# The first unit's row maxima moved from GpSimd to VectorE, sent in two transfers instead of four, and four max products moved behind the start of the attention loop

## The chip, the cores and the metric

The kernel runs on one NeuronCore of a Trainium2 chip. Its engines are TensorE (PE; PEld is its weight load), VectorE (DVE), ScalarE (ACT), GpSimd (POOL) and SyncE (SP), which here only issues DMA transfers. The metric is the device time of one execution in microseconds: the median of the timed runs.

## The reference

A transformer block whose two normalizations are modulated by a condition vector. 2048 rows of 512 numbers, 32 heads of 16 numbers, one key and one value head shared by all of them, and an MLP of width 1376:

```python
mod = silu(c) @ w_mod                       # sa, ca, ga, sb, cb, gb
h = layernorm(x) * (1 + ca) + sa
q, k, v = h @ wq, h @ wk, h @ wv            # k and v have one head
p = softmax(einsum("bhqd,bkd->bhqk", q, k) * Dh ** -0.5)
x = x + ga * (einsum("bhqk,bkd->bhqd", p, v) @ wo)
h = layernorm(x) * (1 + cb) + sb
x = x + gb * (gelu(h @ w1 + b1) @ w2 + b2)
```

## The kernel before, in words

**Units.** The 2048 query rows are cut into 8 blocks of 256, the 32 heads into 8 groups of 4. A block and a group are a *unit*; there are 64, and a block's 8 units come one after the other (`units`, line 469). The queries of unit u lie in one of four buffers `qst` (`load_q`, line 473, brings them with eight transfers; six for the first four units). The partitions 0 to 63 of the buffer hold two heads (s = 0), the partitions 64 to 127 the other two (s = 1), so that two products run beside each other on the two halves of the array.

**Max products.** The softmax subtracts each row's maximum within the score product itself: two partitions of each half of `qst` (48, 49 and 112, 113) hold the negated share of the maxima, high and low part, against keys' rows that hold -1. So the maxima have to be known before a unit's score products. For them the scores are computed a first time: `Max.step` (line 505) issues one product of 128 queries with 512 keys into a bank of PSUM `m` (three banks in turn) and VectorE reduces it to one maximum per row (line 517). A unit has 32 such products; the two halves s have lists of their own. When the last one of a unit is reduced, `put_max` (line 536) lets VectorE reduce over the four key blocks and transpose (lines 565 and 566), GpSimd arrange the turned numbers in rows (four small operations, line 560) and split them into a high and a low part (lines 133 and 140), and sends the four rows into `qst` (line 555).

**Prologue.** Normalization, keys, values and the first queries are computed for all rows. Max products of units 0 and 1 are put between the other products by the table `SLOTS`: each entry gives a number of products and the names of jobs behind them (`rows`: modulation rows on TensorE; `wq n`: a quarter of the query weights split by ScalarE and GpSimd, `prep_wq`, line 336; `load`: `load_q(2)`). `FIRST_MAX` is the order of the first products; unit 0's 48th in that order is its last. While the prologue runs, whatever is put off with `later` is done at once. Then `while mp.done < lead[0]` adds products until `lead[0]` = 32 + 4 * `LEAD_0` are done, and `keep_warm(WARM[3])` adds idle products, which nobody reads.

**Loop.** Each unit has eight steps K, taken in pairs: an iteration has a step X = K and a step Y = K + 1. In the first half the score products of X are mixed with max products of later units and, if there is one, with a batch of another job (late query projections, and later the output projection and the MLP); the second half does the same for Y. `sexp` (line 597) computes a score product into one of three banks `e` and ScalarE takes its exponential; `pv` (line 629) multiplies by the values into the bank `v`. Where there is a batch, the first half takes max products of s = 1, the second those of s = 0. A counter `clock` goes up by four in an iteration, so by 16 in a unit: two counts after each half step. Jobs put off with `later(n, fn)` are issued when it has moved on by n: the maxima's reduction at the next count that is 1 mod 4, the gather one count later, the transfers four counts after the reduction (`MAX_WAIT`). Preparation of weights (`prep_w1` and others: load, split on GpSimd, store through SyncE) takes a step at each iteration's end.

**How many max products.** `lead[u]` is how many are to be done when unit u begins: 32 * (u + 1) + 24 from unit 8 on, and in a straight line from `lead[0]` to `lead[8]` before. Each iteration issues the even number that comes nearest to the line: 8 in all iterations before the change. `load_q(u + 1)` is issued as soon as half of unit u's products are reduced.

**Order.** Every engine, SyncE too, executes its instructions in the order in which the program issues them. An instruction that waits holds all behind it on that engine.

Of the kernel before, what the change touches and what calls it, by code (L numbers as in the profile page):

```python
# [14 lines left out]
P = 128  # L15
# [4 lines left out]
GELU_R = 0.044715 ** 0.5  # L20

LEAD = 6
LEAD_0 = 6
FIRST_MAX = ((0, 0), (1, 0), (0, 1), (1, 1), (0, 2), (0, 3), (1, 2), (1, 3))
SLOTS = ((2, "keys 1", "keys 1"), (2, "keys 1", "keys 1"), (2, "low 1", "heads 2"), (2, "heads 2", "k 1"), (1, "warm"), (1, "heads 2"), (2, "heads 2", "v 0"),
# [4 lines left out]
MAX_WAIT = (1, 4)  # L30
QBUFS = 4
PREP = 4
# [9 lines left out]
SOON = 6  # L42
GROUP = 4
NORM_WAIT = 6
WARM = (4, 16, 2, 5)
MOD_WAIT = 3
AHEAD = 4.5

# [1 line left out]
def raw(ap):  # L50
    return ap.bitcast(F32)
# [3 lines left out]
def adaln_mqa_mlp(  # L55
# [15 lines left out]
    nc = tc.nc  # L71
# [25 lines left out]
    def pad(pool, nbytes, name):  # L97

        nc.gpsimd.memset(pool.tile([P, nbytes // 4], F32, name=name), 0.0)
# [27 lines left out]
    def ebank():  # L127
        turns[0] += 1
        return dict(tag=f"e{turns[0] % 3}", bufs=1)

    def split(dst_h, dst_l, src, eng_h, eng_l, between=None):
        if eng_h is nc.gpsimd:
            eng_h.tensor_scalar(out=dst_h, in0=src, scalar1=1.0, scalar2=0.0, op0=ALU.mult, op1=ALU.add)
        elif eng_h is nc.scalar:
            eng_h.copy(dst_h, src)
        else:
            eng_h.tensor_copy(out=dst_h, in_=src)
        if between:
            between()
        eng_l.tensor_tensor(out=dst_l, in0=src, in1=raw(dst_h), op=ALU.subtract)  # L140
# [7 lines left out]
    def later(n, fn):  # L148
        if draining[0]:
            fn()  # L150
        else:
            pending.append((clock[0] + n, fn))
# [130 lines left out]

    idles = []

    def keep_warm(n, **place):

        for k in range(n):
            if k == 0 or not place:
                ps = psum.tile([P, BQ], F32, name=f"idle{len(idles)}", **(place or dict(tag="m", bufs=3)))  # L290
                idles.append(ps)
            nc.tensor.matmul(ps, wkH[:, 0, :], wkH.rearrange("p k n -> p (k n)"), start=True, stop=True)

    def mod_rows(ps, k, wm):

# [19 lines left out]
    wkH = pro.tile([P, KD, P], F32R, name="wkH")  # L315
# [32 lines left out]
    bigH = att.tile([P, NB - 1, KD, BQ], F32R, name="bigH", tag="bigH")  # L348
# [8 lines left out]
    def stats1(b, between=None):  # L357
        mv, rs = ln_stats(xts[b], pro, QT, between)
        nm = pro.tile([P, QT], F32, name=f"nm{b}", tag="nm", bufs=2)
        if b:  # L360
            nc.gpsimd.tensor_tensor(out=nm, in0=mv[:, :, 0], in1=rs, op=ALU.mult)
            nc.gpsimd.tensor_scalar(out=nm, in0=nm, scalar1=-1.0, scalar2=0.0, op0=ALU.mult, op1=ALU.add)
        hts_stats[b] = mv, rs, nm

    def xhat1(b, eng):

        mv, rs, nm = hts_stats[b]
        xt = xts[b]
        for t in range(QT):
            if eng is nc.scalar:  # L370
                nc.scalar.activation(xt[:, t, :], xt[:, t, :], AF.Identity, scale=rs[:, t:t + 1], bias=nm[:, t:t + 1])
            else:
                eng.tensor_scalar(out=xt[:, t, :], in0=xt[:, t, :], scalar1=mv[:, t, 0:1], scalar2=rs[:, t:t + 1],
                                  op0=ALU.subtract, op1=ALU.mult)
            yield

    def turn1(b, d):
        ps = psum.tile([P, BQ], F32, name=f"tp{b}_{d}", **ebank())
        for t in range(QT):
            nc.tensor.transpose(ps[:, t * P:(t + 1) * P], xts[b][:, t, d * P:(d + 1) * P], ident)  # L380
        tps[b, d] = ps

    def mod1(b, d, eng_h, eng_l, between=None):
        hH, hL = hts[b]
        h32 = pro.tile([P, BQ], F32, name=f"h32_{b}_{d}", tag="h32", bufs=4)
        nc.scalar.activation(h32, tps.pop((b, d)), AF.Identity, scale=ca1[:, d:d + 1], bias=sa[:, d:d + 1])
        split(hH[:, d, :], hL[:, d, :], h32, eng_h, eng_l, between)
# [142 lines left out]
    placed = set()  # L530
# [5 lines left out]
    def put_max(u, mx):  # L536

        T = blocks[units[u][0]][1] // P  # L540
        qst = qsts[u]
        mm = mms[u % 2]
        turned = att.tile([P, 32], F32, name=f"turned{u}", tag="turned", bufs=2)
        if u == 0:
            pad(att, 256, "pad7")
        mt = att.tile([4 * T, P], F32, name=f"mt{u}", tag="mt", bufs=2)
        mh = att.tile([4 * T, P], F32R, name=f"mh{u}", tag="mh", bufs=2)
        ml = att.tile([4 * T, P], F32R, name=f"ml{u}", tag="ml", bufs=2)

        def send():  # L550
            for s in range(2):
                for r, src in ((48, mh), (49, ml)):
                    dst = qst[64 * s + r:64 * s + r + 1].rearrange("p j (t n) -> p (j t) n", n=P)
                    ring = nc.scalar if u == 0 and s else nc.sync
                    ring.dma_start(out=raw(dst), in_=raw(src[2 * T * s:2 * T * (s + 1), :].unsqueeze(1)))
            placed.add(u)

        def gather():
            for g in range(0, P, 32):
                nc.gpsimd.tensor_scalar(out=mt[:, g:g + 32], in0=turned[g:g + 4 * T, :], scalar1=1.0, scalar2=0.0,  # L560
                                        op0=ALU.mult, op1=ALU.add)
            split(mh, ml, mt, nc.gpsimd, nc.gpsimd)

        def reduce():
            nc.vector.tensor_reduce(out=mm[:, :4 * T], in_=mx, axis=AX.X, op=ALU.max)
            nc.vector.transpose(out=turned, in_=mm)  # L566
            later(MAX_WAIT[0], gather)
            later(MAX_WAIT[1], send)


        if NQ <= u < NQ + 2:
            reduce()
        else:
            later((0 - clock[0]) % 4 + 1, reduce)
# [661 lines left out]
    first = [sum(size[:u]) for u in range(NU + 1)]  # L1236
    mp = Max()

    def chunk(n):
        for _ in range(n):  # L1240
            mp.step(mp.done % 2)

    act, dve, pool = nc.scalar, nc.vector, nc.gpsimd

# [16 lines left out]
    def run(job, n=99):  # L1261
        for _ in range(n):
            if next(job, True):
                return

    def heads(b):

        for d in range(KD):
            turn1(b, d)
            mod1(b, d, pool if d == 1 else act, dve if b == 1 and d > 1 else pool)  # L1270
            if (b, d) == (2, KD - 1):
                load_mods(3)
            yield

    def keys(b):
        for i, _ in enumerate(kv_products(b)):
            if i == KD - 1:
                kv_out(b)
            yield
# [8 lines left out]
    def q_group():  # L1288
        for i in range(KD):
            next(projections[0])  # L1290
            if i == KD - 1:
                next(projections.pop(0))
            yield

    def warm():
        keep_warm(WARM[2], tag="x")
        yield

    def one(fn, *args):
        fn(*args)  # L1300
        yield
# [13 lines left out]
    turn1(0, 3)  # L1315
    keep_warm(WARM[0])
    mod1(0, 1, pool, dve, lambda: stats1(1))
# [3 lines left out]
    rows = xhat1(1, act)  # L1321
# [17 lines left out]
    def last_h(t):  # L1339
        if t == QT - 1:  # L1340
# [5 lines left out]
    run(xhat1(2, act))  # L1346
    run(xhat1(3, pool))
    keep_warm(WARM[1])
    work = {"keys 1": keys(1), "heads 2": heads(2), "heads 3": heads(3), "q 1": q_group(), "keys 2": keys(2), "keys 3": keys(3),
            "v 0": one(v_out, 0), "v 1": one(v_out, 1), "v 2": one(v_out, 2), "v 3": one(v_out, 3), "rows": late_rows(),  # L1350
            "low 1": one(low_k, 1), "low 2": one(low_k, 2), "low 3": one(low_k, 3), "k 1": one(repeat_k, 1), "k 2": one(repeat_k, 2), "k 3": one(repeat_k, 3), "load": one(load_q, 2), "warm": warm(),
            "wq 1": one(prep_wq, 1), "wq 2": one(prep_wq, 2), "wq 3": one(prep_wq, 3)}
    for n, *names in SLOTS:
        chunk(n)
        for name in names:
            next(work[name])
    assert 0 in placed and len(mods_late) == KD
    draining[0] = False
    nc.gpsimd.tensor_scalar(out=b1r, in0=b1c, scalar1=GELU_R, scalar2=0.0, op0=ALU.mult, op1=ALU.add)
# [9 lines left out]
    for u in range(NQ):  # L1369
        lead[u] = min(first[1] + 4 * LEAD_0 + (lead[NQ] - first[1] - 4 * LEAD_0) * u / NQ, first[u + QBUFS - 1] - 2)  # L1370

# [35 lines left out]
            if units[u][1] == NQ - 1:  # L1407
                put_off(rest(units[u][0], units[u][0] == len(blocks) - 1))

    keep_warm(WARM[3], tag="e2", bufs=1)  # L1410
    behind = None
    bare = [False]
    for u in range(NU):
        for K in range(0, steps[u], 2):
            goal = lead[u] + (lead[u + 1] - lead[u]) * (K + 2) / steps[u]
            goal = min(goal, first[u + QBUFS] if u + QBUFS < NU else first[NU])
            n = max(0, 2 * round((goal - mp.done) / 2))
# [165 lines left out]
```

## Time and profile before

| | |
|---|---|
| timed runs, us | 1556.4, 1556.62, 1558.17 (median 1556.62) |
| profiled execution, us | 1555.99 |
| its span, us | 1554.1 |
| granted TensorE clock | 1.0 |
| TensorE busy | 1537.9 us, 99% |
| VectorE busy | 1398.3 us, 90% |
| ScalarE busy | 1230.4 us, 79% |
| GpSimd busy | 683.7 us, 44% |
| first score product of the loop | at 75.14 us |

The span goes from the first to the last instruction of the profiled execution; the execution's time is a little longer. A row of the timeline gives start and length in us, engine, line, operation, output and inputs with sizes and the number of instructions merged; in brackets stands how long the engine was idle before and what ended that. SPq and ACTq are transfers issued by SyncE and ScalarE. Rows of the table by stretches give the busy time of PE, PEld, DVE, ACT and POOL (with the number of instructions), then the granted clock, the share of time in which the DMA engines were busy, and GB/s.

### The profile page before, as it was taken

Reading aid. Unit: us, or ns where it says so; the run is one execution under the profiler, and the core shown is the slowest. Engines: PE = TensorE matmul, PEld = TensorE weight load, DVE = VectorE, ACT = ScalarE, POOL = GpSimd, SP = SyncE. Lnnn points to the kernel's source line nnn. Section 1 sums busy time; section 2 is a strip of 40 time slices with the busy share of each in tenths; the row PEclk is TensorE's granted clock in tenths of the full one; section 3 lists DMA queues with packets and bytes.
Section 4 is the critical chain, followed back from the end, with each engine's and each line's share of the span. In section 5 each row is a group of like instructions: output and inputs, shape, how many; then the busy total and the mean of one; then the engine's idle time right before and its main releaser. Section 6 shows DMA issues by size and latency. Waiting matters only on the chain.

```text
span 1554.1 us, 41556 instructions
## 1 busy us (share of the span) xinstructions
PE 1537.9 (99%) x16405; PEld 954.4 (61%) x16405; DVE 1398.3 (90%) x2488; ACT 1230.4 (79%) x2401; POOL 683.7 (44%) x1206
## 2 busy tenths in 40 slices
PE   7999999999999999999999999999999999999999
PEld 4455555567655665557655676556655676566658
DVE  7999999999999999999999999999999999999814
ACT  5577778788877887788877888788877888778874
POOL 5535432867422571246521563235711574046511
PEclk9999999999999999999999999999999999999999
DMA  7226412413030220303112120302212230203141
GB/s 240 102 89 199 151 57 81 130 51 97 18 105 26 72 68 28 103 19 109 33 51 79 56 87 16 111 26 88 68 30 73 60 101 25 87 28 99 48 150 48
DMA packets 84215, 120.85 MB, mean 78 GB/s; under 512 B 21342, under 2 KB 57438, under 8 KB 83764
## 3 DMA queue, kind: packets, MB, share of 16 engines
q1 hardware_dynamic: 84004, 118.18, 23.7%
q8 instruction: 130, 2.13, 0.6%
q14 instruction: 65, 0.53, 0.1%
q10 hardware_dynamic: 16, 0.00, 0.0%
HBM read 90.87 MB, written 26.74 MB: 76 GB/s over the span
## 4 chain that ended last, share of the span: by engine, by line
PE 86%; DVE 8%; issue 3%; POOL 2%; DMA 1%; ACT 0%; SPq 0%; POOLq 0%; DVEq 0%
PE acc L638 29%; PE m L512 23%; PE e L617 16%; PE w1ps L198 8%; DVE mx L517 6%; PE w2ps L198 2%; PE w2ps L188 2%; DMA xt<-in_A_x_dram 1%; PE w1ps L188 1%; PE wops L198 1%; PE tp L198 1%; PE qps L198 1%; PE kps L165 1%; DVE st L823 0%; DVE x L816 0%
## 5 line engine op out<-in xcount | busy, mean ns | idle before, releaser
L517 DVE TENSOR_REDUCE mx<-m 128x1 f32<-128x512 f32 x2048 | 1270.6, 682 | 86.6 <-PE m L512 65.1
L621 ACT ACTIVATE p<-e 128x512 f32<-128x512 f32 x2048 | 1098.8, 598 | 255.1 <-PE e L617 112.0
L512 PE MATMUL m<-ks,qst 64*128 64x512 f32 x2048 | 836.7, 429 | 2.0 <-DVE mx L517 0.6
L617 PE MATMUL e<-qst,ks 64*128 64x512 f32 x2048 | 740.2, 412 | 0.0
L638 PE MATMUL acc<-p,va 128*32 128x256 f32 x8192 | 548.0, 385 | 0.0
L512 PEld LDWEIGHTS m<-ks,qst 64*128 64x128 f32 x2048 | 368.2, 184 | 205.1 <-DVE mx L517 173.5
L617 PEld LDWEIGHTS e<-qst,ks 64*128 64x128 f32 x2048 | 359.6, 184 | 89.3 <-ACT p L621 62.5
L638 PEld LDWEIGHTS acc<-p,va 128*32 128x32 f32 x8192 | 214.0, 109 | 213.9 <-issue 110.9
L198 PE MATMUL w1ps<-h2H,w1t 64*128 64x256 f32 x1232 | 235.5, 287 | 0.0
L560 POOL TENSOR_SCALAR mt<-turned 8x32 f32<-8x32 f32 x256 | 53.1, 208 | 399.9 <-DVE turned L566 387.9
L198 PEld LDWEIGHTS w1ps<-h2H,w1t 64*128 64x128 f32 x1232 | 186.0, 185 | 28.9 <-DVE mx L517 14.8
L198 PE MATMUL w1ps<-h2L,w1t 64*128 64x256 f32 x616 | 169.3, 275 | 0.0
L198 PE MATMUL w2ps<-w2H,gH 64*128 64x512 f32 x274 | 120.3, 439 | 0.0
L198 PEld LDWEIGHTS w1ps<-h2L,w1t 64*128 64x128 f32 x616 | 114.1, 185 | 0.0
L198 PE MATMUL w2ps<-w2L,gH 64*128 64x512 f32 x274 | 107.5, 392 | 0.0
L198 PE MATMUL w2ps<-w2H,gL 64*128 64x512 f32 x274 | 106.9, 390 | 0.0
L975 POOL TENSOR_SCALAR tt<-tt 128x256 f32<-128x256 f32 x77 | 31.0, 402 | 131.5 <-ACT tt L974 96.5
L140 POOL TENSOR_TENSOR gL<-z,gH 128x256 fp32r<-128x256 f32 x77 | 57.0, 741 | 6.4
L976 POOL TENSOR_TENSOR tt<-tt,z 128x256 f32<-128x256 f32 x77 | 56.7, 736 | 6.4
L986 POOL TENSOR_TENSOR z<-tt,z 128x256 f32<-128x256 f32 x77 | 56.4, 732 | 6.0
L985 POOL TENSOR_TENSOR tt<-tt,z 128x256 f32<-128x256 f32 x77 | 56.5, 733 | 0.0
L198 PEld LDWEIGHTS w2ps<-w2H,gH 64*128 64x128 f32 x274 | 50.4, 184 | 6.7 <-DVE ot L1038 2.5
(193 smaller groups left out, 1503.5 us busy)
## 6 DMA issues: line engine op xcount, KB each, us to landing
w1t<-dw SPq DMA_DIRECT2D x82, 512.0 KB
qst<-dq SPq DMA_DIRECT2D x384, 32.0 KB
do<-oc SPq DMA_DIRECT2D x62, 128.0 KB
dw<-w1s SPq DMA_DIRECT2D x11, 512.0 KB
xt<-in_A_x_dram SPq DMA_DIRECT2D x4, 1024.0 KB
dq<-qH SPq DMA_DIRECT2D x16, 256.0 KB
dq<-qL SPq DMA_DIRECT2D x16, 256.0 KB
x<-in_A_x_dram SPq DMA_DIRECT2D x8, 512.0 KB
```

Of the source, the lines that this page charges most:

```text
L140: eng_l.tensor_tensor(out=dst_l, in0=src, in1=raw(dst_h), op=ALU.subtract)
L188: nc.tensor.matmul(ps, a, b_, start=first_, stop=last_)
L198: ins = nc.tensor.matmul(ps, a[rows], b_[rows], start=first_ and s == 0, stop=last_ and s == 1)
L512: nc.tensor.matmul(m, qsts[u][rows, j, t * P:(t + 1) * P], ks[rows, kc * 512:(kc + 1) * 512], start=True, stop=True)
L517: nc.vector.tensor_reduce(out=self.mx[u][:, i, kc:kc + 1], in_=m, axis=AX.X, op=ALU.max)
L560: nc.gpsimd.tensor_scalar(out=mt[:, g:g + 32], in0=turned[g:g + 4 * T, :], scalar1=1.0, scalar2=0.0, op0=ALU.mult, op1=ALU.add)
L617: nc.tensor.matmul(e, ks[rows, kt * P:(kt + 1) * P], rhs, start=True, stop=True)
L621: ins = nc.scalar.activation(dst, e, AF.Exp, scale=0.25)
L638: ins = nc.tensor.matmul(accs[u][32 * cidx:32 * cidx + 32, :], va[:, kt, :], rhs, start=kt == 0, stop=kt == NKT - 1)
L976: nc.gpsimd.tensor_tensor(out=tt, in0=tt, in1=z, op=ALU.mult)
L985: nc.gpsimd.tensor_tensor(out=tt, in0=tt, in1=z, op=ALU.mult)
L986: nc.gpsimd.tensor_tensor(out=z, in0=tt, in1=z, op=ALU.add)
```

## The change

Unit 0's rows no longer go to GpSimd: `place_first` lets VectorE make the four copies, the high and the low part directly behind the transpose. The high parts of both halves go in one transfer (two partitions, 64 apart), the low parts in another, both from SyncE; before, SyncE and ScalarE issued two each. `LEAD_0` is 5 instead of 6, so that `lead[0]` is 52 instead of 56, and `SLOTS` has two products fewer. `prep_wq(3)` is moved up in the table, into the slot of products 45 and 46. The 48th product (`wide`) takes a bank of `e` instead of `m`. The idle products in front of the loop are four instead of five, go to the bank `v` and read `bigH` instead of `wkH`.

```diff
-LEAD_0 = 6
+LEAD_0 = 5
-         (2, "q 1", "rows"), (2, "v 3", "wq 2"), (2, "rows"), (2, "rows"), (2, "rows", "wq 3", "load"))
+         (2, "q 1", "rows"), (2, "v 3", "wq 2", "wq 3"), (2, "rows"), (2, "rows"), ("rows", "load"))
-WARM = (4, 16, 2, 5)
+WARM = (4, 16, 2, 4)
...
-    def keep_warm(n, **place):
-
+    def keep_warm(n, src=None, **place):
+
+        src = wkH.rearrange("p k n -> p (k n)") if src is None else src
...
-            nc.tensor.matmul(ps, wkH[:, 0, :], wkH.rearrange("p k n -> p (k n)"), start=True, stop=True)
+            nc.tensor.matmul(ps, src[:, :P], src, start=True, stop=True)
...
-                    ring = nc.scalar if u == 0 and s else nc.sync
-                    ring.dma_start(out=raw(dst), in_=raw(src[2 * T * s:2 * T * (s + 1), :].unsqueeze(1)))
+                    nc.sync.dma_start(out=raw(dst), in_=raw(src[2 * T * s:2 * T * (s + 1), :].unsqueeze(1)))
+            placed.add(u)
+
+        def place_first():
+            for g in range(0, P, 32):
+                nc.vector.tensor_copy(out=mt[:, g:g + 32], in_=turned[g:g + 4 * T, :])
+
+            def send_row(r, src):
+                dst = qst[r:r + 65:64].rearrange("p j (t n) -> p (j t) n", n=P)
+                nc.sync.dma_start(out=raw(dst), in_=raw(src.unsqueeze(1)))
+
+            split(mh, ml, mt, nc.vector, nc.vector, lambda: send_row(48, mh))
+            send_row(49, ml)
             placed.add(u)
...
             nc.vector.transpose(out=turned, in_=mm)
+            if u == 0:
+                place_first()
+                return
             later(MAX_WAIT[0], gather)
             later(MAX_WAIT[1], send)
...
+    wide = [False]
+
     def chunk(n):
         for _ in range(n):
-            mp.step(mp.done % 2)
+            mp.step(mp.done % 2, **(ebank() if wide[0] and mp.done % 2 else {}))
...
-    for n, *names in SLOTS:
-        chunk(n)
-        for name in names:
-            next(work[name])
+    for i, slot in enumerate(SLOTS):
+        wide[0] = i == len(SLOTS) - 3
+        for part in slot:
+            if isinstance(part, int):
+                chunk(part)
+            else:
+                next(work[part])
...
-    keep_warm(WARM[3], tag="e2", bufs=1)
+    keep_warm(WARM[3], bigH[:, 0, 0, :], tag="v")
```

## The prediction

> **What bounds the kernel now.** I read the page first, then the order of time around the end of the prologue, then SyncE's queue through the first units.
>
> ```profile
> span 1554.1 us, 41556 instructions
> PE 86%; DVE 8%; issue 3%; POOL 2%; DMA 1%; ACT 0%; SPq 0%; POOLq 0%; DVEq 0%
> L517 DVE TENSOR_REDUCE mx<-m 128x1 f32<-128x512 f32 x2048 | 1270.6, 682 | 86.6 <-PE m L512 65.1
> ```
>
> The chain of work that ended last lies on TensorE for 86% of the span and on VectorE for 8%. VectorE's large task is one reduction (0.68 us) per max product, 2048 of them; the change leaves that number as it is and moves four of them. The profiled execution took 1555.99 us, 1.9 more than its span; the median of the timed runs is 1556.62. A measurement of this kernel can tell about 0.2% (3.1 us) from no change.
>
> The seam between prologue and loop, in the timeline of all engines (start, length, engine, line, operation):
>
> ```profile
> 67.05 2.48 DVE L517 TENSOR_REDUCE mx<-m 128x1 f32<-128x512 f32 x4 [1.05 <-PE m L512]
> 67.30 0.98 PE L512 MATMUL m<-ks,qst 64*128 64x512 f32 x2
> 68.22 1.44 POOL L343 TENSOR_TENSOR wqL<-wqf,wqH 128x256 fp32r<-128x256 f32 x2
> 69.56 0.19 DVE L565 TENSOR_REDUCE mm<-mx 128x8 f32<-128x32 f32 x1
> 69.78 0.21 DVE L566 STREAM_TRANSPOSE turned<-mm 128x32 f32<-128x32 f32 x1
> 69.92 5.14 DVE L517 TENSOR_REDUCE mx<-m 128x1 f32<-128x512 f32 x8
> 71.19 0.29 POOL L133 TENSOR_SCALAR mh<-mt 8x128 fp32r<-8x128 f32 x1
> 71.50 0.69 SPq L555 DMA_DIRECT2D qst<-mh  x1
> 72.29 0.61 SPq L555 DMA_DIRECT2D qst<-ml  x1
> 72.96 0.59 ACTq L555 DMA_DIRECT2D qst<-ml  x1
> 73.32 0.50 PE L512 MATMUL m<-ks,qst 64*128 64x512 f32 x1 [0.32 <-DVE mx L517]
> 73.75 1.47 PE L292 MATMUL idle<-wkH 128*128 128x512 f32 x5
> 75.14 0.49 PE L617 MATMUL e<-qst,ks 64*128 64x512 f32 x2
> 75.91 6.67 DVE L517 TENSOR_REDUCE mx<-m 128x1 f32<-128x512 f32 x11 [0.85 <-PE m L512]
> ```
>
> Products 45 to 48 are reduced back to back from 67.05 to 69.53, and then unit 0's maxima are complete. VectorE reduces and turns them (to 69.99), GpSimd arranges and splits them, and four transfers write the rows. Meanwhile eight more products (49 to 56) pass; the last is held by VectorE (73.32), five idle products follow, and at 75.14 the loop's first score product starts. So two paths meet at 75.14: TensorE behind VectorE's eight reductions, and the rows.
>
> ```profile
> 73.50:73.75 0.25, 0.25 (x2) 0.01 (x2) 0.25 (x1) 0.16 (x1) 0.00 (x0) 1.00 0.03 8
> 74.00:74.25 0.25, 0.25 (x2) 0.18 (x2) 0.25 (x1) 0.25 (x2) 0.16 (x1) 1.00 0.02 6
> 74.25:74.50 0.25, 0.25 (x3) 0.20 (x2) 0.25 (x2) 0.08 (x1) 0.25 (x1) 1.00 0.01 2
> ```
>
> These are rows of the table by stretches; the last column is GB/s. The last transfer (issued 72.96, 2 KB) moves at 74.0 to 74.5 (6 and 2 GB/s for 0.25 us each make 2 KB). No wait for it is shown at 75.14. From the start of an issue to a landed row are thus 1.5 to 2.2 us; I take 1.8.
>
> **The change, part by part.**
>
> *Rows on VectorE.* Four copies (8x32), one cast and one subtraction (8x128) follow the transpose. No row shows these shapes; the nearest, by form:
>
> ```profile
> L282 DVE COPY csb<-cs 128x128 f32<-128x128 f32 x1 | 0.2, 228 | 0.0
> L310 DVE COPY sa<-modc 128x4 f32<-128x4 f32 x1 | 0.2, 163 | 0.3 <-PE modc L301 0.3
> L329 DVE TENSOR_TENSOR wkL<-wkv,wkH 128x64 fp32r<-128x64 f32 x1 | 0.2, 226 | 0.0
> ```
>
> A copy lasts between 0.163 and 0.228; overlapped (the reduction at 69.92 starts 0.14 after the transpose) four take 0.4 to 0.8. Cast and subtraction take 0.23 each, the latter perhaps 0.3. Sum 0.9 to 1.4; I take 1.2, near the dependent end. The high part is then ready at about 70.9 instead of 71.48 (71.19 + 0.29), and its one transfer goes out then; the second starts 0.8 later behind it on SyncE (as 72.29 behind 71.50), at 71.7 instead of 72.96, and lands at 73.2 to 73.9.
>
> *TensorE there.* Product 49's reduction moves to 69.99 + 1.2 = 71.2 and ends at 71.9. Product 52 uses its bank, so it starts at 71.9. From product 56 to the first score product were 1.82 us (73.32 to 75.14) with five idle products; one less takes off about 0.25 (1.47 for five, overlapped). Score products then start at 71.9 + 1.6 = 73.5; with the rows' 73.5 beside it I take 73.6: **-1.5 us**. Were the VectorE work 0.8, it would be -1.9; with GpSimd in the way, -0.8.
>
> GpSimd can be in the way because `prep_wq(3)` moves up one slot: its two subtractions (1.44 by the row at 68.22) follow those of `prep_wq(2)`, from 69.66 to 71.1, just as VectorE makes the rows. Two such operations have met before:
>
> ```profile
> 30.25 0.69 DVE L140 TENSOR_TENSOR bigL<-h,bigH 128x512 fp32r<-128x512 f32 x1 [0.27 <-ACT bigH L135]
> 31.58 1.07 DVE L140 TENSOR_TENSOR bigL<-h,bigH 128x512 fp32r<-128x512 f32 x1 [0.64 <-ACT bigH L135]
> 30.27 1.83 POOL L140 TENSOR_TENSOR bigL<-h,bigH 128x512 fp32r<-128x512 f32 x1
> ```
>
> VectorE's first took 0.69; its second, begun while GpSimd's long one ran, 1.07: 0.4 more. So one meeting is priced at 0.4, up to 0.7 for two; half of one is in my 73.6. [...]
>
> *Costed at nothing.* Product 48 in a score bank: TensorE moves on 0.5 sooner, but VectorE reduces it no earlier (67.05 x4 is unbroken); without that cover nothing is lost either. Idle products reading `bigH`, in bank v: v is empty until `acc`. ScalarE's two transfers go; nothing on the path stood behind them.
>
> *Four products into the loop.* `lead[0]` falls from 56 to 52 and `lead[8]` stays 312, so each of units 0 to 7 should do 32.5. Rounded to even numbers per iteration (two steps, 8 products), two iterations do 10 instead of 8: the first of unit 2 and the first of unit 6.
>
> ```profile
> 124.56:147.39 22.83, 22.83 (x243) 13.56 (x241) 21.17 (x37) 17.69 (x34) 12.90 (x18) 1.00 0.61 201
> ```
>
> ```profile
> 125.90 0.39 PE L198 MATMUL qps<-bigH,wqL 64*128 64x512 f32 x1
> 126.13 0.39 PE L198 MATMUL qps<-bigL,wqH 64*128 64x512 f32 x1
> ```
>
> The first row is unit 2's stretch: 22.83 us, so 5.7 per iteration, with TensorE full and VectorE 21.17, 93%; the other two show products of one half of the array 0.23 us apart. Two more products cost TensorE 2 x 0.23 us, if nothing runs beside them on the other half, and VectorE 2 x 0.60 (11 reductions in 6.67). VectorE's 1.7 us of slack are spread over four iterations, and only three banks buffer. Bounds 0.46 and 1.2 per iteration, I take 0.7: **+1.4 us** (0.9 to 2.4).
>
> *Rows of units 1 to 6 come later.* A unit's maxima are reduced at the next count of the loop's clock (four counts an iteration, 16 a unit) that is 1 mod 4. With 24 products of lead the last max product of the next unit falls in the first iteration's second half, and the reduction is at clock 5, the gather at 6, the rows' transfers at 9 of 16. With 20 to 22 it falls into the second iteration's second half: reduction 9, gather 10, transfers 13, 5.7 us later, three clocks (4.3 us) before the next unit. At unit 7 the ten products bring it back. `load_q` moves too, from clock 10 (behind the transfers) to 12 (ahead of them). Mostly that is covered:
>
> ```profile
> 107.86 0.67 SPq L555 DMA_DIRECT2D qst<-mh  x1
> 109.91 0.57 SPq L555 DMA_DIRECT2D qst<-ml  x1
> 120.22 0.39 PE L617 MATMUL e<-qst,ks 64*128 64x512 f32 x1
> ```
>
> Unit 2's last row was issued at 109.91; 5.7 later is 115.6, landed by 117.8, and its first score product is at 120.22: 2.4 us to spare. `load_q` has no wait there and runs ahead, in the time that SyncE used to wait for the rows. Not so before unit 4, where the late modulation fills the queue:
>
> ```profile
> 158.35 0.50 SPq L1178 DMA_DIRECT2D dw<-w1s  x1
> 158.95 0.65 SPq L555 DMA_DIRECT2D qst<-mh  x1
> 161.41 0.57 SPq L555 DMA_DIRECT2D qst<-ml  x1
> 162.03 1.87 SPq L483 DMA_DIRECT2D qst<-dq  x3
> 166.75 0.35 SPq L1178 DMA_DIRECT2D dw<-w1s  x1
> 165.87 0.39 PE L617 MATMUL e<-qst,ks 64*128 64x512 f32 x1
> ```
>
> In before's times: SyncE is free at 158.9, then sends the next `dw` (0.45), then `load_q(6)`, eight issues from 162.03 to 166.70, 4.7 us: 159.4 to 164.1. Only then come the rows. Their fourth issue starts 2.1 after the first (as 107.86 to 109.91), at 166.2, and lands at 167.7 to 168.4. The first score product of unit 4 reads it and wants it at 165.87, with all of TensorE queued behind it, then ScalarE and VectorE: **+2.0 us** (0 to 2.5).
>
> Sum: -1.5 + 1.4 + 2.0 = **+1.9 us** (bounds -1.0 and +4.1): 1557.9 beside the profiled 1555.99, and 1558.5 beside the median 1556.62, which I forecast.
>
> **The rivals.** *No stall at unit 4*: if `load_q(6)` gets out sooner, or lands behind the rows, the third term is nil: -0.1, 1556.5. For it speaks that the queue there is one long chain whose times I shift by hand; against it, that SyncE works in order. *Late rows at every start* (the slower side): the transfers of units 1, 2, 3, 5 and 6 also leave one iteration later. It decides once a landing takes more than 4.6 us from its issue (115.6 to 120.22). For it speaks the DMA share of 0.61 in unit 2's stretch; against it the 2.2 us bound. At 1 us over, five starts give 5 us: 1563.5. *Faster*: the extra products fall into VectorE's slack at 0.46 an iteration, no start is late, and the loop starts 1.9 sooner: -1.0, 1555.6; for more than 0.2% the 1.9 us around the span would have to go as well, as the second queue does, which no row supports. That the change does not do what it says would be unread maxima as many as before (56 at the loop's start): no change, 1556.6; the diff's numbers exclude it.
>
> **How the numbers follow.** Forecast 0.50; no stall 0.29; late rows everywhere 0.15; faster variants 0.06, of which 0.03 pass 0.2%. Slower by over 0.2% (above 1559.7): the 0.15 and 0.03 of the forecast's upper end, 0.18. Within: 0.79. The range goes from 1554.6, below the faster variant, to 1561.4, half-way into late rows. The forecast's own range is 1557 to 1560.
>
> **What would show it.** The first score product at 73.6 (73.2 to 74.4); VectorE's six small operations 1.2 us in sum; ten reductions in the first iterations of units 2 and 6 and 0.7 us more there; the rows' transfers 5.7 us later in units 1 to 6; TensorE idle about 2 us ahead of unit 4's first score product, ended by a transfer. The prediction is wrong if that gap is missing or stands at every unit, or if the loop's start gains less than 0.8.

## The result, and the profile after

The changed kernel takes 1563.38 us (median of 6 runs, 1562.49 to 1565.36) against 1556.71 us before (6 runs, 1556.05 to 1558.17): a ratio of 1.0044 with a 95% interval of 1.0031 to 1.0057. It is slower by 0.4%, outside the predicted range of 1554.6 to 1561.4. The profiled execution took 1563.1 us with a span of 1561.3, so 7.2 us more than before (1554.1).

From the page of the kernel after: the span, the chain by engine, and two groups (busy us, mean ns | idle us ahead of them, and what ended most of it).

```profile
span 1561.3 us, 41554 instructions
PE 89%; DVE 7%; DMA 2%; POOL 1%; issue 1%; ACT 0%; SPq 0%; POOLq 0%; DVEq 0%
L518 DVE TENSOR_REDUCE mx<-m 128x1 f32<-128x512 f32 x2048 | 1270.4, 681 | 89.7 <-PE m L513 67.9
L632 PE MATMUL e<-qst,ks 64*128 64x512 f32 x2048 | 740.5, 412 | 2.9 <-DMA qst<-ml 2.9
```

VectorE's reductions are as many and as long as before. New is the last row: the loop's score products waited 2.9 us in all for a transfer of `ml`, and DMA has 2% of the chain instead of 1%.

The seam between prologue and loop, in the timeline of the kernel after:

```profile
66.50 2.48 DVE L518 TENSOR_REDUCE mx<-m 128x1 f32<-128x512 f32 x4 [1.05 <-PE m L513]
67.69 2.85 POOL L344 TENSOR_TENSOR wqL<-wqf,wqH 128x256 fp32r<-128x256 f32 x4
69.24 0.21 DVE L578 STREAM_TRANSPOSE turned<-mm 128x32 f32<-128x32 f32 x1
69.49 1.53 DVE L560 COPY mt<-turned 8x32 f32<-8x32 f32 x4
71.05 0.22 DVE L137 CAST mh<-mt 8x128 fp32r<-8x128 f32 x1
71.30 0.28 DVE L140 TENSOR_TENSOR ml<-mt,mh 8x128 fp32r<-8x128 f32 x1
71.51 2.46 DVE L518 TENSOR_REDUCE mx<-m 128x1 f32<-128x512 f32 x4
72.06 0.53 SPq L564 DMA_DIRECT2D qst<-ml  x1
72.24 0.50 PE L513 MATMUL m<-ks,qst 64*128 64x512 f32 x1 [1.28 <-DVE mx L518]
73.79 0.50 PE L632 MATMUL e<-qst,ks 64*128 64x512 f32 x2
```

VectorE makes the rows in 2.06 us (69.45 to 71.51), of which the four copies take 1.53; GpSimd's subtractions for weight pieces 2 and 3 run until 70.54, beside them. TensorE stands still for 1.28 us ahead of product 52. The first score product starts at 73.79 (75.14 before). But the prologue ahead of the change was 0.55 sooner in this execution: product 45, the first of the four, started at 65.96 and before at 66.51 (its reduction 66.50 and 67.05). Executions differ by more than that: product 45 starts at 65.71 in run e7 and at 67.16 in run e5 below, whose kernels are the same up to there. What the change moved is told by the time from product 45 to unit 0's first sum (`acc`), before and after:

```profile
66.51 0.50 PE L512 MATMUL m<-ks,qst 64*128 64x512 f32 x2
78.88 1.07 PE L638 MATMUL acc<-p,va 128*32 128x256 f32 x16
```

```profile
65.96 0.50 PE L513 MATMUL m<-ks,qst 64*128 64x512 f32 x2
77.84 1.07 PE L653 MATMUL acc<-p,va 128*32 128x256 f32 x16
```

That is 12.37 us before and 11.88 after: **0.49 us sooner**. Up to the first score product it is 0.80 sooner (8.63 and 7.83 us); the other 0.31 is lost between the two.

Then the table by stretches of the kernel after (PE, PEld, DVE, ACT, POOL busy; granted clock; DMA share; GB/s):

```profile
74.00:75.00 1.00, 1.00 (x8) 0.73 (x6) 0.26 (x1) 0.67 (x2) 0.00 (x0) 0.59 0.22 64
75.00:76.00 1.00, 1.00 (x6) 0.59 (x4) 1.00 (x3) 1.00 (x3) 0.00 (x0) 0.50 0.14 35
76.00:77.00 1.00, 1.00 (x6) 0.97 (x5) 1.00 (x3) 1.00 (x3) 0.00 (x0) 0.50 0.29 66
77.00:78.00 1.00, 1.00 (x9) 0.45 (x10) 1.00 (x3) 0.90 (x3) 0.00 (x0) 0.71 0.19 49
```

Behind TensorE's stop the granted clock falls to 0.50. A row of 1 us at 0.59 was at half speed for (1.00 - 0.59) x 2 = 0.82 us; with two whole rows and 0.58 us of the last that makes 3.40 us. Before, it is 1.00 throughout.

The largest loss lies at unit 4's start. SyncE's queue and TensorE there, in the timeline of the kernel after:

```profile
159.76 2.75 SPq L484 DMA_DIRECT2D qst<-dq  x3
162.55 0.44 SPq L486 DMA_DIRECT2D qst<-dz  x1
163.09 1.81 SPq L484 DMA_DIRECT2D qst<-dq  x3
164.94 0.43 SPq L486 DMA_DIRECT2D qst<-dz  x1
165.49 0.65 SPq L555 DMA_DIRECT2D qst<-mh  x1
167.54 0.57 SPq L555 DMA_DIRECT2D qst<-ml  x1
169.28 0.47 PE L632 MATMUL e<-qst,ks 64*128 64x512 f32 x1 [2.93 <-DMA qst<-ml]
```

`load_q(6)` (eight issues, 159.76 to 165.37) goes ahead of unit 4's rows; the last row is issued at 167.54, and the score product starts 1.74 us later, after TensorE stood still for 2.93 us. Behind this stop too the clock is halved, for 3.42 us by the same sum:

```profile
169.00:170.00 1.00, 0.72 (x6) 0.69 (x8) 0.00 (x0) 0.21 (x1) 0.00 (x0) 0.87 0.93 358
170.00:171.00 1.00, 1.00 (x8) 0.93 (x6) 0.69 (x1) 0.85 (x2) 0.00 (x0) 0.50 1.06 420
171.00:172.00 1.00, 1.00 (x8) 0.33 (x10) 0.77 (x2) 0.25 (x2) 0.00 (x0) 0.50 0.67 262
172.00:173.00 1.00, 1.00 (x12) 0.39 (x8) 0.61 (x1) 0.97 (x2) 0.00 (x0) 0.50 0.08 25
173.00:174.00 1.00, 1.00 (x13) 0.49 (x6) 0.04 (x1) 0.37 (x1) 0.00 (x0) 0.92 0.00 0
```

A unit is eight half steps, each from one first `acc` to the next. By stretches, units 1, 3 and 5 (from `acc` to `acc`, so that the wait at unit 4's first score product lies in unit 3's stretch), before:

```profile
101.78:124.56 22.78, 22.78 (x242) 13.53 (x240) 21.11 (x37) 17.70 (x34) 12.89 (x18) 1.00 0.56 178
147.39:170.22 22.83, 22.83 (x243) 13.58 (x241) 21.14 (x37) 17.70 (x34) 11.72 (x18) 1.00 0.52 166
193.04:215.45 22.41, 22.38 (x234) 12.75 (x232) 21.01 (x36) 17.49 (x35) 11.65 (x16) 1.00 0.22 75
```

and after:

```profile
100.63:124.73 24.10, 24.10 (x245) 13.93 (x243) 22.33 (x38) 18.21 (x35) 12.87 (x18) 1.00 0.53 176
147.71:175.28 27.57, 24.64 (x243) 14.45 (x241) 21.54 (x37) 17.86 (x33) 11.66 (x18) 0.94 0.50 164
198.11:221.72 23.61, 23.39 (x236) 13.08 (x234) 22.31 (x38) 18.07 (x36) 11.67 (x16) 1.00 0.21 72
```

Unit 3's stretch is 4.74 us longer, unit 5's 1.20, unit 1's 1.32. In units 1 and 5 it is the last two half steps, each 3.30 instead of 2.84 or 2.71: score products run ahead of the sums, so the ten-product iterations of units 2 and 6 show there, with another 0.15 in unit 2. That is 0.93 + 0.15 + 1.19 = 2.27 us. The other 0.38 of unit 1 is its fifth half step, where a copy of late projections on VectorE starts later. So the 7.2 us are: earlier prologue -0.55, start -0.49, ten products +2.27, unit 1's fifth half step +0.38, unit 4 +4.74, later units +0.85 (0.64 of it in one half step each of units 21, 28 and 60), and -0.1 in unit 0.

### The profile page after: what moved, and what is told of

It reads as the page before. It is cut to its first block, busy times and chain, and to the rows that moved or that the text cites. A ratio compares the mean times of both kernels' runs of the same rounds, so it can differ in the third digit from the quotient of the medians.

```text
span 1561.3 us, 41554 instructions
## 1 busy us (share of the span) xinstructions
PE 1542.3 (99%) x16404; PEld 956.2 (61%) x16404; DVE 1400.8 (90%) x2494; ACT 1230.8 (79%) x2401; POOL 682.3 (44%) x1200
## 4 chain that ended last, share of the span: by engine, by line
PE 89%; DVE 7%; DMA 2%; POOL 1%; issue 1%; ACT 0%; SPq 0%; POOLq 0%; DVEq 0%
PE acc L653 30%; PE m L513 25%; PE e L632 16%; PE w1ps L198 8%; DVE mx L518 6%; PE w2ps L198 2%; PE w2ps L188 2%; PE wops L198 1%; DMA xt<-in_A_x_dram 1%; PE w1ps L188 1%; PE qps L198 1%; PE tp L198 1%; PE kps L165 1%; DVE st L838 0%; PE wops L188 0%
```

## The experiments

My theory after the result: **the shorter lead costs the time** (through the wait at unit 4, the ten-product iterations and a half clock behind each stop), and VectorE's rows are worth little. Rivals: VectorE's rows themselves cost it; the start is slow because GpSimd works beside the copies.

**The lead undone** (e1) in the changed kernel.

```diff
-LEAD_0 = 5
+LEAD_0 = 6
```

> The kernel after, with LEAD_0 back at 6: 56 products stand in front of the loop again, every iteration has eight, and the rows of units 1 to 6 go out at clock 9. Theory L (the lead): the loss of 6.7 us lies in the loop, 4.7 us at the start of unit 4 (2.9 us of waiting for its rows, and 1.8 us of TensorE at half its granted clock behind that) and 2.5 us in the two iterations of ten products. Then all of it goes, and only the start differs from before: VectorE makes the rows in 2.1 us ahead of eight reductions, so the loop starts 0 to 1.5 us later: 1556.5 to 1558.5. Theory V (VectorE): the loss comes from the rows on VectorE and TensorE's stop and half clock in front of the loop; then this stays above 1561.

1560.65 us against 1556.72, 1.0021 (1.0012 to 1.003). The wait at unit 4 and the iterations of ten are gone, as the theory wants, but the time is between the two expectations, for the start is later: from product 45 to the first sum 15.63 us (12.37 before). Now the rows stand ahead of eight reductions on VectorE, product 52 waits 1.30 us, and the clock is halved for 6.8 us instead of 3.4. So at equal lead VectorE's rows, with all that came with them, cost time.

**The lead alone** (e2), in the kernel before.

```diff
-LEAD_0 = 6
+LEAD_0 = 5
```

> The kernel before with LEAD_0 at 5 and nothing else: the rows of unit 0 stay on GpSimd with four transfers, 52 products stand in front of the loop. Theory L: the wait at unit 4 and the iterations of ten products come with it, +7.2 us, and the start gains 0.5 to 1.5 us from four reductions less: 1562.4 to 1563.4. Theory V: 1555.5 to 1557.5.

1563.19 us, 1.004 (1.0027 to 1.0053): the lead alone loses as much as the whole change. Unit 4's start takes 7.37 + 3.13 us instead of twice 2.84, the half steps of ten products 3.29 to 3.31. At the loop's start GpSimd's rows come late, in the timeline of this kernel:

```profile
72.24 1.42 PE L292 MATMUL idle<-wkH 128*128 128x512 f32 x5
74.74 0.56 PE L617 MATMUL e<-qst,ks 64*128 64x512 f32 x2 [1.07 <-DMA qst<-ml]
```

Even so, the first sum comes 11.76 us after product 45 (66.71 to 78.47), 0.61 sooner than before the change. The changed kernel's 0.49 is thus no more than what the lead gives alone; VectorE's rows add nothing to it as long as GpSimd works beside them.

**Rows reduced at once** (e3) for units 1 to 9, so that they go out ahead of `load_q`; all else as changed.

```diff
-        if NQ <= u < NQ + 2:
+        if 1 <= u < NQ + 2:
```

> The kernel after, but units 1 to 9 (before: 8 and 9 only) reduce their maxima as soon as the last product is reduced, not at the next clock that is 1 mod 4. Their rows then go out at clock 10 instead of 13, on SyncE ahead of the load of a later unit's queries instead of behind it. Theory L: the wait at unit 4 goes with its 4.7 us, the iterations of ten stay: 1558.6. If the rows are late for another reason than their place in SyncE's order (GpSimd, or the transfers themselves), a wait of 1 us or more stays: above 1560. Theory V: 1563.4.

1559.45 us, 1.0018 (1.001 to 1.0027). No wait at unit 4 (half steps 2.84); the iterations of ten stay. The order on SyncE is the cause of that wait: with unit 4's rows from 159.95 on, ahead of `load_q(6)`, it is gone, and with it 3.9 us of the medians. SyncE's queue in this kernel:

```profile
159.95 0.67 SPq L555 DMA_DIRECT2D qst<-mh  x1
162.11 0.57 SPq L555 DMA_DIRECT2D qst<-ml  x1
163.21 1.94 SPq L484 DMA_DIRECT2D qst<-dq  x3
```

**The stop at unit 4 filled** (e4) with idle products; the rows come as late.

```diff
+            if u == 4 and K == 0:
+                keep_warm(13, bigH[:, 0, 0, :], tag="m", bufs=3)
```

> The kernel after, with 13 idle products (3.0 us, read by nobody) in front of unit 4's first step, where TensorE otherwise waits 2.9 us for the rows. Theory H: the products behind the wait last 0.62 instead of 0.39 us because TensorE stood still and its granted clock fell to 0.50; kept busy, the clock stays at 1.0 and about 1.8 us go: 1561.6. Rival T: they are slow for the transfers that move at over 350 GB/s just then, or for something else that the idle products do not change: 1563.4, with the same 0.62.

1562.64 us, 1.0039 (1.0025 to 1.0052). The granted clock stays at 1.00 there and unit 3's stretch is 26.0 us instead of 27.57: the half clock cost 1.57 us. By stretches:

```profile
168.00:170.00 2.00, 2.00 (x10) 1.43 (x8) 0.00 (x0) 0.00 (x0) 0.00 (x0) 1.00 0.01 3
170.00:172.00 2.00, 2.00 (x19) 1.38 (x22) 1.38 (x3) 1.08 (x2) 0.00 (x0) 1.00 1.05 404
```

The median fell by 0.7 only, between the two expectations. In the profiled execution the prologue was 1.12 us later than in the kernel after (product 45 at 67.08), which hides most of the gain there.

**Weight piece 3 back in the last slot** (e5), to take GpSimd from beside the copies.

```diff
-         ... (2, "v 3", "wq 2", "wq 3"), (2, "rows"), (2, "rows"), ("rows", "load"))
+         ... (2, "v 3", "wq 2"), (2, "rows"), (2, "rows"), ("rows", "wq 3", "load"))
```

> The kernel after, with the split of the last quarter of the query weights (wq 3) back in the prologue's last slot, so that GpSimd has no subtraction to do while VectorE makes unit 0's rows. Theory G: the four 8x32 copies took 1.53 us in the kernel after because GpSimd's subtractions ran beside them; alone they take 0.7 or less, TensorE's wait at product 52 falls from 1.28 to about 0.4 us, its clock stays at 1.0 there and the loop starts 0.9 us sooner: 1562.4. Rival: four copies that start on four different groups of partitions take 0.38 us each by themselves: 1.5 us again, 1563.4.

1564.18 us, 1.0052 (1.0039 to 1.0065). It tells nothing of the question: ScalarE's casts had nothing to wait for, so GpSimd's subtractions ran beside the copies all the same (1.55 us).

**The short lead for all units, rows at once in all** (e6, e7, e8: the changed kernel; the same with piece 3 moved back; the kernel before, there with `LEAD_0 = 5` too).

```diff
-LEAD = 6
+LEAD = 5
-        if NQ <= u < NQ + 2:
+        if u:
```

> The kernel after with a lead of 20 products for all units (LEAD 5 beside LEAD_0 5) and all units' maxima reduced as soon as they are complete. No iteration has ten products, and no rows stand behind a load of queries; the four products left out in front are done at the loop's end. If iterations of ten cost 2.2 us beyond the rows-at-once run (1559.45), and their four products cost less than 1 us at the end: 1557 to 1558. Rival: a deferred product costs what it costs wherever it is done: 1559.5.

> The run before this one (lead of 20 for all, rows at once) with wq 3 back in the last slot as well. If both theories hold the gains add up, about 0.9 us less than that run: 1556 to 1557, no slower than before. If the copies are slow by themselves: equal to that run.

> The kernel before (rows of unit 0 on GpSimd, four transfers, wq 3 last) with a lead of 20 for all units and rows at once. It tells what the lead alone is worth without its side effects: the loop starts 0.6 us sooner as in the run with LEAD_0 alone, and nothing is given back: 1555.5 to 1556.5. Where VectorE's rows gain something of their own, the run before this one lies below it.

1573.56 (1.0112, 1.0098 to 1.0126), 1574.05 (1.0115, 1.0101 to 1.0129) and 1574.9 us (1.0115, 1.01 to 1.013): all three missed by 16 to 18 us. Units 1 to 8 have neither wait nor ten products, but from unit 9 on the third half step of most units is 0.15 to 0.6 us longer; why was not followed. As the kernel with GpSimd's rows loses the same, VectorE's rows have no part in it.

**GpSimd made free** (e9) while VectorE makes the rows: the splits of pieces 2 and 3 moved ahead of the last block's values.

```diff
-         (0, "v 2"), (2, "q 1"), ...
+         (0, "v 2", "wq 2", "wq 3"), (2, "q 1"), ...
-         ... (2, "v 3", "wq 2", "wq 3"), ...
+         ... (2, "v 3"), ...
```

> The changed kernel, with the splits of weight pieces 2 and 3 (ScalarE's casts and GpSimd's four subtractions wqL, 2.85 us) moved ahead, in front of the last block's values, so that GpSimd has nothing to do while VectorE makes unit 1's rows' first four copies. Theory C (the four 8x32 copies took 1.53 us because GpSimd was at work beside them): the copies fall to some 0.2 us each, 0.8 in sum, TensorE's stop ahead of product 52 falls from 1.28 to about 0.5 us, the half clock from 74 to 78 us goes, and the time falls by 0.7 to 2.3 us against the changed kernel's ratio of 1.0044, to about 1561.1 to 1562.7 at a kernel before of 1556.7. Theory S (such a copy takes 0.38 us by itself, as it begins at another partition than it ends at): copies 1.5 us again, the stop and the half clock stay, time 1563.4 within 0.7.

1567.54 us, 1.0073 (1.006 to 1.0085): the time missed, for the projection now waits for these splits (TensorE stands still for 1.03 and 1.47 us ahead of 62.69 and 64.66, with a half clock from 64.0 on). The copies answer the question. By the tile `mt`, shortest, median and longest copy in ns, after:

```profile
L560 DVE COPY mt<-turned x4: 169/278/769, 69.5 to 70.8; 8x32 f32<-8x32 f32 x4
```

and with GpSimd free:

```profile
L560 DVE COPY mt<-turned x4: 169/170/173, 75.1 to 75.7; 8x32 f32<-8x32 f32 x4
```

A copy takes 0.17 us by itself; beside GpSimd's subtractions two of the four took 0.38 and 0.77, and they end 0.03 and 0.12 us after a subtraction ends. The four take 0.72 us instead of 1.53. From product 45 to the first sum are 10.74 us, 1.63 less than before. By what means GpSimd holds a copy up, no run shows.

**Four idle products ahead of product 52** (e10), where TensorE stood still.

```diff
     while mp.done < lead[0]:
+        if mp.done == lead[0] - 1:
+            keep_warm(4, bigH[:, 0, 0, :], tag="v")
         chunk(1)
```

> The changed kernel with four idle products on TensorE ahead of product 52, where it stood still for 1.28 us; 52 itself still waits for VectorE. If the clock's fall to 0.50 from 74 to 78 us came from that stop: the granted clock stays 1.00 from 72 to 78, unit 1's first sum begins about 1.5 us sooner after product 45 (10.4 instead of 11.88) and the time is about 1561.9 at a kernel before of 1556.7. If the half clock has another cause (or the stop is only moved): clock 0.5 again and 1563.4 within 0.7.

1562.9 us, 1.0045 (1.0031 to 1.0058): missed. (The first sum that the expectation means is unit 0's.) The clock is 1.00 from 70 to 80 us as expected, but the first sum comes 11.51 us after product 45, 0.37 sooner and not 1.5: VectorE sets the time there (busy for 1.00 in each row from 75 to 78 us in the kernel after), and TensorE at half clock beside it cost no more than these 0.37 us. (This execution had 6.84 us of half clock in the prologue, ahead of the edit, where the kernel after had none.) The stop at unit 4 was there again, and the clock did not fall behind it, so that unit 3's stretch was 25.76 us instead of 27.57 (timeline, then stretches):

```profile
172.35 0.46 PE L632 MATMUL e<-qst,ks 64*128 64x512 f32 x1 [2.69 <-DMA qst<-ml]
```

```profile
172.00:173.00 1.00, 0.65 (x6) 0.66 (x8) 0.00 (x0) 0.15 (x1) 0.00 (x0) 1.00 0.87 336
173.00:174.00 1.00, 1.00 (x14) 0.59 (x14) 0.91 (x2) 0.94 (x2) 0.00 (x0) 1.00 1.08 426
```

**GpSimd free without the side effect**: the splits are held back by a one-column copy on ScalarE that waits for the last modulation product. Once with rows at once for units 1 to 9 (e11), once with the old lead (e12).

```diff
-         ... (2, "v 3", "wq 2", "wq 3"), ...
+         ... (2, "v 3"), ...
...
+    nc.scalar.copy(att.tile([P, 1], F32, name="hold", tag="hold"), mod_state["ps"][:, :1])
+    next(work["wq 2"])
+    next(work["wq 3"])
```

> The changed kernel with the rows of units 1 to 9 reduced at once (as in the earlier run that took away the wait at unit 4, ratio 1.0018) and the splits of weight pieces 2 and 3 held behind the last product of the modulation (a copy of one column on ScalarE holds its casts back), so that GpSimd has nothing to do while VectorE makes the first unit's rows. If GpSimd beside them is what made the four copies 1.5 us instead of 0.72, the copies are 0.72 here, the first sum begins 10.7 to 11.1 us after product 45 (11.88 in the changed kernel, 12.37 before), no wait at unit 4, the ten-product iterations stay, and the time is 1558.0 to 1559.0 at a kernel before of 1556.2 (ratio 1.0012 to 1.0018): still slower than before. If the held-back weights keep a late projection waiting, a half step of unit 0 or 1 is longer and the gain is lost again.

1558.74 us, 1.0017 (1.0008 to 1.0025), as expected: copies 0.72 us, first sum 10.75 us after product 45, ten products and unit 1's 0.4 us as in the changed kernel. Against e2's 11.76 that is 1.0 us: so much VectorE's rows and the two transfers gain at the short lead once GpSimd is quiet.

> The changed kernel with the lead of 6 steps as before the change (52 + 4 products in front of the loop; ratio 1.0021 with that alone) and the same splits held back. It asks whether the rows on VectorE and the two transfers bring anything once nothing runs beside them. If the loss at the start came from the slow copies and from TensorE's stop: the copies take 0.72 us, the stop is about 0.5 us instead of 1.30, the start is 0.8 to 2.5 us sooner than with the lead of 6 alone, and the time is 1558.1 to 1559.8 (ratio 1.0005 to 1.0016 at 1556.7). If the rows cost the same on VectorE whatever is beside them: 1.0021 again.

1560.35 us, 1.0019 (1.0009 to 1.0029): the time missed, though the copies take 0.72 and the stop 0.47 us. The first sum comes 14.80 us after product 45, 0.83 sooner than in e1 and just within the expectation, and the half clock is back behind the short stop (stretches):

```profile
72.00:74.00 2.00, 1.37 (x3) 0.55 (x3) 2.00 (x4) 1.46 (x5) 1.85 (x3) 1.00 0.01 4
74.00:76.00 2.00, 1.90 (x4) 0.94 (x4) 2.00 (x5) 0.00 (x0) 1.19 (x3) 0.61 0.17 49
76.00:78.00 2.00, 2.00 (x6) 1.16 (x7) 0.55 (x1) 0.00 (x0) 0.00 (x0) 0.50 0.22 49
78.00:80.00 2.00, 2.00 (x10) 1.27 (x9) 1.21 (x3) 1.63 (x4) 0.00 (x0) 0.50 0.00 0
80.00:82.00 2.00, 2.00 (x12) 1.35 (x15) 2.00 (x5) 2.00 (x5) 0.00 (x0) 0.68 0.00 0
```

Of its nine executions, the two with a mean granted clock of 1.000 took 1557.64 and 1558.69 us, the six with 0.998 took 1560.05 to 1561.22: the half clock seems to come in some executions of this kernel and not in others, and that is enough for the miss. At equal lead the rows' 1.2 us on VectorE (70.44 to 71.69) stand ahead of eight reductions that the start waits for anyway, where GpSimd made them beside these.

**The short lead for all units, later units' rows at the usual count**: e11 with `LEAD = 5` (e13), and the kernel before with `LEAD = LEAD_0 = 5`, rows at once for units 1 to 9 in both (e14).

```diff
-LEAD = 6
+LEAD = 5
```

> The run before with rows at once for units 1 to 9 and the splits held back (ratio 1.0017: start 1.6 us sooner, but 2.3 us in ten-product iterations and 0.4 us in unit 1), now with LEAD = 5 as well, so that the four products are never made up and no iteration has ten; units 10 and later reduce their rows at the loop's usual count, as in the changed kernel, not at once as in the earlier run with LEAD = 5. Theory Z (the 2.3 us are only the price of making the four products up, and a lead of 20 costs nothing elsewhere if rows are reduced at the usual count): no half step of 3.30 in units 1 and 5, later units as in the kernel before, 1555.4 to 1556.9 at a kernel before of 1556.4 (ratio 0.9994 to 1.0003). Theory W (with a lead of 20 later units wait for their rows or the rows' work falls beside other work, whatever its count): later half steps are longer and the time is 1562 or more, as with LEAD = 5 before (1.011).

> The kernel before with LEAD = LEAD_0 = 5 and rows at once for units 1 to 9 alone: the same without VectorE's rows. With the lead alone TensorE stood still for 1.07 us ahead of the first score product, for GpSimd's rows. If Theory Z holds, this is 1556.5 to 1558.0 (the wait at the start stays, no ten-product iterations), 1 us behind the other run of this call, and that difference is what VectorE's rows and the two transfers are worth. If W holds, 1562 or more as well.

1636.67 us (1.0515, 1.0489 to 1.0541) and 1636.34 us (1.0509, 1.0489 to 1.0529): Theory W. At the start the first sum comes 10.75 and 11.71 us after product 45, the same 1.0 us for VectorE's rows as above. Units 0 to 8 have no ten products, and unit 9's first sum begins at 278.20 in the first and 279.15 in the second (279.70 before). But from unit 11 on, starts of units wait for rows; the group of score products in the first one's page:

```profile
L632 PE MATMUL e<-qst,ks 64*128 64x512 f32 x2048 | 755.3, 415 | 47.8 <-DMA qst<-ml 47.7
```

24 waits make 47.7 us (the count is from its table of waits), the half clock behind them (mean granted clock 0.985) and what follows the rest of the 80. A lead of 20 products is too short for the usual count, and rows at once cost 17 us. The 2.27 us for making the four products up keep that loss away.

None of these kernels is faster than the kernel before. The bank of the 48th product, the idle products and the number of transfers were not changed on their own.

## Why the prediction was wrong

**The step that failed is unit 4's wait, +2.0 us (0 to 2.5); it was 4.74.** The mechanism was named rightly (rows behind `load_q(6)` on SyncE; run e3 removes it), and landing was 1.74 us from issue against an estimated 1.8. Two sizes were off. The eight issues of `load_q(6)` took 5.6 us, not the 4.7 of before; they ran 2.3 us sooner, and the first three lasted 2.75 instead of 1.87. So the wait was 2.93. And a halved clock behind the stop was not in the sum at all: 1.81 us, of which run e4 gave back 1.57; e10, where the clock did not fall, shows the same.

**Ten-product iterations, +1.4 (0.9 to 2.4): 2.27**, within its bounds at the VectorE end. Each moved product cost 0.57 us, nearly VectorE's 0.60 per reduction; that the slack spread over a unit does not help in the iteration that needs it is the likely reason, not one that a run isolates.

**Start, -1.5 us (-0.8 with GpSimd in the way): -0.49.** With GpSimd free it is -1.62 and -1.63 (e11, e9), so the estimate for the six operations (1.2 us, measured 1.25 in e11) was right for a quiet GpSimd. Beside GpSimd two copies were delayed, by 0.81 us in sum; I had 0.7 for two meetings, but only half of one, 0.2, in the sum. That leaves 0.80 up to the first score product, which is the -0.8 that I gave for GpSimd in the way, beside the -1.5 of the sum. The other 0.31 is the half clock, which was not in the sum: from the first score product to the first sum are 4.05 us, against 3.74 before and 3.73 in e10, where the clock stayed at 1.00. That the first score product started at 73.79, within my 73.2 to 74.4, is luck: the prologue was 0.55 sooner.

**Rows one iteration later: right**; unit 2's last row was issued at 114.55, and no start but unit 4's waited. The rival of late rows at every start did not occur here, and that its 1563.5 is next to the measured 1563.38 is a coincidence; e13 shows such waits 24 times in later units at the same lead.

**At nothing** I put unit 1 and the later units; they cost 0.38 and 0.85. Why is open. The 0.38 is missing in the kernel before with the short lead (e2, e8, e14) and in the changed one with the old lead (e1, e12), and stands in all others; the three longer half steps of units 21, 28 and 60 are in e1, e3 to e5 and e9 to e12, which are all made from the changed kernel, and not in e2.

Sum of the errors: unit 4 +2.7, start +1.0, ten products +0.9, the rest +1.2, less 0.55 for the earlier prologue, together 5.3, which is 7.2 less the predicted 1.9. The chances failed with it: I gave 0.79 to a change within 0.2%, and the 1561.4 at the upper end had no term for the clock.

What stays open is which stop is followed by a half clock (the last section has a part of the answer). That the lead causes most of the loss is shown by e2 and e3; that GpSimd slows the copies, by e9 and e11.

## What to carry to other kernels

A lead in front of a loop is bought at the price of the engine that paces both sides (here 0.57 to 0.6 us a product): four products less gained 0.61 us at the start (e2) and cost 2.27 in the loop. What it feeds, the order in the issuing queue at each later start, is to be counted with it (here 3.9 us of the medians at unit 4, e3). Work moved to a pacing engine stands ahead of that engine's other work (here 1.2 us ahead of eight reductions, e12), and took longer here where the engine that it left worked beside it (the copies 1.53 us instead of 0.72). A stall of a full TensorE is to be priced with the chance of a halved clock behind it (here 1.57 us at unit 4).

## What the runs showed of the hardware

The half clock comes in pieces of one length: 3.40 us at the start and 3.42 at unit 4 in the kernel after; in e12 the last four rows make 1.56 + 2.00 + 2.00 + 1.28 = 6.84 us of half speed, two pieces. The length of the stop does not decide: the clock fell after 0.47 (e12), 1.28 and 2.93 us (after), and not after 1.07 (e2) or 2.69 us (e10).

The pieces also begin on a grid. In the kernel after they begin at 74.18 and 169.74, 95.56 us apart, which is 28 times 3.413; in e13 the 13 stretches of half clock in the loop begin, as far as the rows of the timeline tell, at whole multiples of 3.413 us from one another (780.8, 1497.5 and 1524.8 among them, 210 and 8 steps apart). Counted from each trace's own pieces (at 169.80 in e2, from 61.84 on in e10), a point of the grid, at 74.24 and at 171.07, cuts the stops of e2 and e10 in two, while the three that were followed lie whole between two points. That is not all: the stop of 0.99 us ahead of unit 0 in e14 lies between two points as well (its pieces give 72.73 and 76.14) and was not followed. So neither the length of a stop nor its place on the grid decides alone; what else does was not measured.
